# A linear-attention and two-MLP kernel: second w3 tile turned earlier, no weight tile begun in five steps, max product at full height

## The chip, the cores and the metric

The kernel runs on one core of one Trainium2 chip. The metric is the device time of one execution in microseconds; before the change it is 998.01 us, the median of 3 runs (996.71 to 998.25).

## The reference

```python
def phi(x):                                     # x: 4 x 8 x 576 x 64
    proj = np.einsum('bhsd,df->bhsf', x, w_phi) # f = 128
    proj = proj - np.max(np.abs(proj), axis=-1, keepdims=True)
    return np.concatenate([np.exp(proj), np.exp(-proj)], axis=-1)
q_p, k_p = phi(q), phi(k)
kv = np.einsum('bhsf,bhsd->bhfd', k_p, v)
z = np.sum(k_p, axis=2)
num = np.einsum('bhsf,bhfd->bhsd', q_p, kv)
den = np.einsum('bhsf,bhf->bhs', q_p, z)[..., None] + 1e-06
x = (num / den).transpose(0, 2, 1, 3).reshape(2304, 512)
h = ((x @ w1) * (x @ w2)) @ w3                  # 512x1024, 512x1024, 1024x1024
x = h @ w_out                                   # 1024 x 512
out = np.maximum(x @ w_in, 0.0) ** 2 @ w_out2   # 512x2048, 2048x512
```

The inputs of the attention are float32; the six MLP weights lie in DRAM as float64.

## The kernel before, in words

**Number forms.** A float32 product is made of three passes of a rounded form: a value is split into a high part (rounded by ScalarE, L142) and a low part (the rest, on VectorE or GpSimd, L143), and high x high, low x high and high x low are summed in PSUM (`passes`, `wide`). So a 512-wide contraction over 4 parts is 12 products. A float64 weight tile of 128x512 is decoded by integer work: its raw words are loaded by a DMA that SP issues (L99), ScalarE scales the high word (L106), VectorE makes the float's bits in four instructions (L108, L111; L115, L118), GpSimd adds (L123), and most tiles are then split (ScalarE L131, GpSimd L133). The generator `decoding` yields between these, so that the caller places them among other work.

**Attention.** 16 pairs of heads (`todo`, four batches by four pairs) run through a software pipeline: the loop over t issues, for every name in the list SLOT, one step of a pair that is t plus that step's offset. START is the same for the first slots. With `manual_schedule` the order in which the code issues is the order on each engine. The table `once` holds steps that run in one slot only; a step with offset -1 there runs in slot 15, with 0 in slot 16 (the pairs' last slot of work is 15; in slot 16 the last pair's `out` products and quotients remain). In a pair, `project_q` (L376) makes the projections of the queries in `pq`, 128 features x 1152 tokens in three banks. `max_q` takes maxima over blocks of 32 with a transposition within 32x32 squares (L383) into `m1`, 36 columns; `max_rows` transposes that on TensorE (L391) to 36 rows of `pm`; `max_parts` ends the maximum (L396), splits it, and two DMAs write its 1152 values as high and low row into `mrow`, a tile of two partitions. `minus_q` (L409) then adds a product of `minus`, 2 rows x 128 columns of -1, and the two rows of `mrow`, to each bank, so that every feature has its token's maximum taken off, and ScalarE takes the exponentials. In SLOT `minus_q` stands behind `turn_q1` or, in the last slots, `turn_w3`, and before `values1` (`pkv`, L428).

**First network.** The products with w3 and w_out are folded into one matrix first: for each of 8 chunks, two w3 tiles are turned on TensorE (`turn_weights`, L171), split (`keep`), and multiplied with w_out (`Fold.product`, L787); the split result `w3o` (`done`) then serves `yp` (L830). The 40 steps of the first network are 2 groups x 5 blocks of tokens (two of 512, one of 256, two of 512) x 4 chunks. A step makes `pa` and `pb` (x with w1 and w2), copies `a` (L902), multiplies (L910), splits, and issues the previous step's `yp`. Folds lie in steps 0 to 7. The first half of fold 0 was turned in slot 15 (`turn_w3`), the second is turned in step 0. The next block's x is loaded in a block's second step and split in three portions: part 0 in the third step, parts 1 and 2 and then 3 in the fourth (L143 on `c`). So steps 8 to 11 and 28 to 31 are the 256-wide block, with the splits of the 512-wide parts that follow in steps 10, 11 and 30, 31.

**Second network.** Step j of 16 in each block makes `ph` (x with w_in), on ScalarE and VectorE the squared ReLU (L971, L973; split L979, L981), and the products with w_out, `op` (L848), of the step before. In the first step the last block of the first network is emptied from PSUM too (`evict_second`, L816).

**Weights.** From slot 15 on `prefetch` loads raw tiles, and in each step of the MLPs `beat.rest(n)` finishes the tiles in hand and begins n new ones; their decode instructions stand between the step's own at `beat.one()` and behind it. The table `many` gives n by step index, 1 where it says nothing; room in the tile pool can hold a tile back (`begin`).

Of the kernel before, what the change touches and what calls it, by code (L numbers as in the profile page):

```python
# [9 lines left out]
F32 = mybir.dt.float32  # L10
F32R = mybir.dt.float32r
# [6 lines left out]
P = 128  # L18
C = 4
TAIL = 64  # L20
LEFT = 20
RIGHT = 13
# [11 lines left out]
tail_values/0  # L34
""".split()
SLOT = """
load_kq product_b project_k0 keep_values x_load project_q project_k1 less_max_k0 max_q turn_k out00 max_rows x_split0 max_parts w-1 store_x less_max_k1 x_split2 out01 exp_k0 x_split1 keep00 w1 high_k out10 keep01 turn_q0 out11 w1 keep_q0 project_k2 denominators0 keep10 w0 keep11 low_k less_max_k2 values0 gate turn_w3 exp_k1 denominators1 x_split3 exp_k2 w0 w0 w0 turn_q1 reciprocals keep_q1 minus_q product_a0 exp_q0 values1 exp_q1 turn_tails keep_tails split_q split_w3 low_tail low_q product_a1 quotients keep_a load_v tail_values
""".split()


# [1 line left out]
def attention_then_mlps(ctx: ExitStack, tc: tile.TileContext, q, k, v, w_phi, w1, w2, w3, wo, wi2, wo2, out):  # L42
    nc = tc.nc
    B, H, S, D = q.shape
# [17 lines left out]
    def unit(dtype, shape, name):  # L62
        return units.tile([P] + shape, dtype, tag="u", bufs=LEFT, name=name)
# [23 lines left out]
    def done_t(name):  # L87
        room_t[home_t.pop(name, 0)] += 1

    turn, room_t, home_t = [0], [2, 2], {}  # L90


    def decoding(src, name, got):
# [75 lines left out]
    def turn_weights(ps, w):  # L169
        for j in range(4):  # L170
            nc.tensor.transpose(ps[:, j * P:(j + 1) * P], w[:, j * P:(j + 1) * P], ident)  # L171
# [26 lines left out]
    with ExitStack() as actx:  # L198
        att = actx.enter_context(tc.tile_pool(name="att", bufs=2, side="right"))
        ps = actx.enter_context(tc.tile_pool(name="ps", bufs=3, space=PSUM))  # L200

        def bank(name, tag="t", bufs=3):
            return ps.tile([P, 512], F32, tag=tag, bufs=bufs, name=name)
# [2 lines left out]

        vs_t = [att.tile([P, 2, C, D + 1], F32, bufs=1, tag=f"vs{i}", name=f"vs{i}") for i in range(VS)]
        vt_t = [att.tile([P, NPR, 2, D + 1], F32, bufs=1, tag=f"vt{i}", name=f"vt{i}") for i in range(2)]
        for t in vs_t:
            nc.gpsimd.memset(t, 1.0)  # L210
        for t in vt_t:
# [167 lines left out]

        def max_q(z):  # L380

            z["m1"] = att.tile([P, 2 * nb], F32, tag="m1", name=f"m1_{z['nm']}")
            nc.vector.tensor_reduce(  # L383
                z["m1"].rearrange("p (i n) -> p i n", i=3), z["pv"].rearrange("p i (n r) -> p i n r", r=32),
                AX.X, ALU.max, apply_absolute_value=True, apply_transpose=True,
            )

        def max_rows(z):

            z["pm"] = bank(f"pm_{z['nm']}")[0:2 * nb, 0:P]  # L390
            nc.tensor.transpose(z["pm"], z["m1"], ident)  # L391

        def max_parts(z):
            pm = z["pm"]
            m = att.tile([2 * nb, 32], F32, tag="m", name=f"m_{z['nm']}")
            nc.vector.tensor_reduce(m, pm.rearrange("p (a r) -> p r a", a=4), AX.X, ALU.max)  # L396
            mh = att.tile([2 * nb, 2, 32], F32R, tag="mh", name=f"mh_{z['nm']}")
            nc.vector.tensor_copy(mh[:, 0], m)
            nc.vector.tensor_tensor(out=mh[:, 1], in0=m, in1=mh[:, 0].bitcast(F32), op=ALU.subtract)
            z["mrow"] = att.tile([2, 2 * S], F32R, tag="mrow", bufs=1, name=f"mrow_{z['nm']}")  # L400
            for s in range(2):
                nc.sync.dma_start(
                    z["mrow"][s:s + 1].bitcast(F32).rearrange("s (k r) -> s k r", r=32), mh[:, s].bitcast(F32)
                )
# [136 lines left out]
        beside += [decoding(*w3_of(i), w3s) for i in range(2)]  # L541
        beside.append(iter(()))
        load_kq(0)
        minus = att.tile([2, P], F32R, bufs=1, name="minus")
        nc.vector.memset(minus.bitcast(F32), -1.0)
        wst = att.tile([D, F], F32, bufs=1, name="wst")
        nc.sync.dma_start(wst, w_phi)
        wss = att.tile([P, 2, F], F32R, bufs=1, name="wss")
# [58 lines left out]
            first["g"] = unit(F32R, [2, 512], "g_0_0")  # L607
            split(first["g"], first["g32"], nc.vector)

        def turn_w3():  # L610
            first["w3T"] = unit(F32R, [2, 512], "w3T_0_0")
            first["pw3"] = bank("pw3_0_0")
            turn_weights(first["pw3"], w3s[0])

        once = {
            "turn_w3": (-1, turn_w3), "split_w3": (-1, lambda: split(first["w3T"], first["pw3"], nc.vector)),
            "x_load": (-3, lambda: load_x(0)),
            "product_a0": (-1, lambda: first_product("a", 0, range(KD - 1))),
            "product_a1": (-1, lambda: first_product("a", 0, range(KD - 1, KD))), "keep_a": (-1, first_a),
# [41 lines left out]
        return pool.tile([P, 512], F32, tag=tag, name=name)  # L661


    free = {"u": LEFT - 17, "w": RIGHT}
    home, given = {}, []

    def take(dtype, shape, name):
# [89 lines left out]
    class Fold:  # L757
# [4 lines left out]

        def turn(self):
            for g in range(2):
                if self.kc + g == 0:
                    continue
                self.ps[g] = bank_of(pre, "pre", f"pw3_{self.kc}_{g}")
                turn_weights(self.ps[g], w3s[2 * self.kc + g])
                done_t(w3_of(2 * self.kc + g)[1])

        def keep(self):
            for g in range(2):
                if g not in self.ps:
                    self.t.append(first["w3T"])
                    continue
                t = take(F32R, [2, 512], f"w3T_{self.kc}_{g}")
                split(t, self.ps[g], nc.vector)
                self.t.append(t)
# [19 lines left out]
    HG = NG // 2  # L798
    steps = [(grp, at, k) for grp in range(2) for at in range(len(order)) for k in range(HG)]
    folds = {i: i for i in range(NG)}  # L800
    many = {0: 3, 1: 3, 2: 2, 3: 2, 4: 2, 5: 2, 6: 2, 37: 2, 38: 2, 39: 2}
    mlp2 = mains + [tail]

    def evict_first(b, n, yp):
# [59 lines left out]
    with tc.manual_schedule(engines=mine):  # L864
# [5 lines left out]
        for s, (grp, at, k) in enumerate(steps):  # L870
# [23 lines left out]
                    blk.part = load_y_at(y_part, b, n, "yp")  # L894
            if s == 0:
                g = first["g"]
                beat.one()
            else:
                pa = bank_of(pre, "pre", f"pa_{b}_{c}")
                wide(pa, n, w12[2 * c], blk.cs)  # L900
                a_sb = lunit(F32, [512], f"a_{b}_{c}", "t", 2)
                nc.scalar.copy(a_sb[:, 0:n], pa[:, 0:n])  # L902
                pb = bank_of(pre, "pre", f"pb_{b}_{c}")
                wide(pb, n, w12[2 * c + 1], blk.cs)
                if at == B:
                    give(w12[2 * c], w12[2 * c + 1])
                if k == HG - 1:
                    col_split(x_in[nb_], nn, f"c{s}_{nb_}", [1, 2])
                g32 = lunit(F32, [512], f"g32_{b}_{c}", "g32", 2)
                nc.vector.tensor_tensor(out=g32[:, 0:n], in0=pb[:, 0:n], in1=a_sb[:, 0:n], op=ALU.mult)  # L910
                g = lunit(F32R, [2, 512], f"g_{b}_{c}", "g", 3)
                nc.scalar.activation(g[:, 0, 0:n], g32[:, 0:n], AF.Copy)  # L912
                beat.one()
                nc.vector.tensor_tensor(
                    out=g[:, 1, 0:n], in0=g32[:, 0:n], in1=g[:, 0, 0:n].bitcast(F32), op=ALU.subtract
                )
                if k == HG - 1:
                    nxt = col_split(x_in[nb_], nn, f"c{s}_{nb_}", [3])
                    give(*coming)
                    if nb_ == B and following[0] == 1:  # L920
                        give(xt)
# [27 lines left out]
        for at, (b, n) in enumerate(mlp2):  # L949
            cs, nt = nxt, n // P  # L950
            ops = None
            for j in range(NR):
# [43 lines left out]
                if j == NR - 2 and at < B:  # L996
                    col_split(x_in[nb_], nn, f"y{at}_{nb_}", [0])
                beat.tail()
                beat = beat.rest(1)
        last_product(prev)  # L1000


# [26 lines left out]
```

## Time and profile before

| | |
|---|---|
| median of 3 runs | 998.01 us (996.71 to 998.25) |
| the profiled execution | 996.72 us |
| its span, first to last instruction | 994.9 us |
| TensorE products, busy | 971.9 us, 98% |
| TensorE weight loads, busy | 813.8 us, 82% |
| VectorE, ScalarE, GpSimd, busy | 574.4, 412.0 and 253.8 us |
| mean granted TensorE clock | 0.992 |

Attention fills the span to about 225 us, the first network to about 587, the second the rest. The profile is of one execution; every row names an engine, the line of the kernel, the output and inputs of the instruction, and how many like it follow one another. In brackets stands the idle time of the engine just before, and what ended it. A row's length reaches from the start of its first instruction to the end of its last; products overlap, so the next row of the same engine can start before that end.

### The profile page before, as it was taken

The numbers are of one execution on the slowest core, as the hardware profiler recorded it, in microseconds if no ns is written. First come the engines' busy times: TensorE is split into PE (matmuls) and PEld (weight loads), VectorE is DVE, ScalarE is ACT, GpSimd is POOL, SyncE is SP. The second block draws the span as 40 slices with busy tenths as digits, with TensorE's granted clock in tenths as the row PEclk, the third lists the DMA queues.
The fourth block names the chain that finished last, engine by engine and source line by source line (L and its number), as shares of the span: only waits on it lengthen the run. The fifth ranks groups of instructions, "written<-read, shape, count | busy, mean of one in ns | idle before, by whom it ended". The sixth has DMA issues, their size and how long they took to land.

```text
span 994.9 us, 13026 instructions
## 1 busy us (share of the span) xinstructions
PE 971.9 (98%) x4944; PEld 813.8 (82%) x4944; DVE 574.4 (58%) x907; ACT 412.0 (41%) x785; POOL 253.8 (26%) x238
## 2 busy tenths in 40 slices
PE   7999999998999999999999989999999999999997
PEld 6888888886888888888888868888888888888896
DVE  5888888878765586467694398733223222322332
ACT  5887777763332343333332233423123222322322
POOL 3455555533321153233341055410000000000000
PEclk9999999998999999999999999999999999999999
DMA  6345444434332154451453343202000200100010
GB/s 175 97 130 141 128 137 124 138 107 148 106 106 66 62 173 131 142 182 64 153 195 127 127 137 97 85 1 85 1 1 21 65 1 0 64 1 1 1 43 22
DMA packets 68559, 89.11 MB, mean 90 GB/s; under 512 B 27984, under 2 KB 53136, under 8 KB 68496
## 3 DMA queue, kind: packets, MB, share of 16 engines
q1 hardware_dynamic: 68496, 88.28, 27.7%
q8 instruction: 39, 0.64, 0.3%
q14 instruction: 24, 0.20, 0.1%
HBM read 69.76 MB, written 18.35 MB: 89 GB/s over the span
## 4 chain that ended last, share of the span: by engine, by line
PE 92%; DVE 5%; issue 1%; DMA 1%; POOL 0%; ACT 0%; DVEq 0%; POOLq 0%
PE op L848 20%; PE ph L177 20%; PE pb L177 9%; PE pa L177 9%; PE yp L830 8%; PE po L452 6%; PE pkv L428 6%; PE pf L787 4%; PE pk L235 2%; PE pq L376 2%; PE pqt L307 1%; PE pq L409 1%; DVE c L143 1%; PE pkv L437 1%; PE pkt L290 1%
## 5 line engine op out<-in xcount | busy, mean ns | idle before, releaser
L848 PE MATMUL op<-w_w,r 128*128 128x512 f32 x864 | 215.6, 397 | 4.4 <-DVE yp L816 4.3
L848 PEld LDWEIGHTS op<-w_w,r 128*128 128x128 f32 x864 | 162.1, 189 | 42.2 <-issue 4.7
L973 DVE SCALAR_TENSOR_TENSOR r<-ph,t 128x512 f32<-128x512 f32 (+1 forms) x80 | 51.1, 638 | 200.2 <-ACT t L971 200.2
L177 PE MATMUL ph<-y,w_w 128*128 128x512 f32 (+1 forms) x768 | 166.2, 365 | 0.0
L177 PEld LDWEIGHTS ph<-y,w_w 128*128 128x128 f32 x768 | 133.3, 188 | 26.3
L971 ACT ACTIVATE t<-ph 128x512 f32<-128x512 f32 (+1 forms) x80 | 44.5, 557 | 223.1 <-PE ph L177 223.1
L830 PE MATMUL yp<-g,w3o 128*128 128x512 f32 (+1 forms) x480 | 107.4, 372 | 0.0
L123 POOL TENSOR_TENSOR dt_w<-dt_w,dy_w 128x512 f32<-128x512 f32 x48 | 63.5, 1323 | 154.8 <-DVE dy_w L118 141.2
L177 PE MATMUL pa<-c,w_w12a 128*128 128x512 f32 (+1 forms) x432 | 96.7, 370 | 3.4 <-DVE c L143 1.7
L830 PEld LDWEIGHTS yp<-g,w3o 128*128 128x128 f32 x480 | 83.6, 188 | 16.0
L177 PE MATMUL pb<-c,w_w12b 128*128 128x512 f32 (+1 forms) x432 | 93.9, 366 | 0.0
L177 PEld LDWEIGHTS pa<-c,w_w12a 128*128 128x128 f32 x432 | 74.9, 188 | 20.3 <-DVE c L143 3.9
L177 PEld LDWEIGHTS pb<-c,w_w12b 128*128 128x128 f32 x432 | 75.2, 188 | 13.4
L981 DVE TENSOR_TENSOR r<-r,r 128x512 fp32r<-128x512 f32 (+1 forms) x80 | 54.3, 679 | 42.7 <-ACT r L979 38.0
L910 DVE TENSOR_TENSOR g<-pb,a 128x512 f32<-128x512 f32 (+1 forms) x39 | 24.8, 636 | 84.8 <-PE pb L177 84.6
L979 ACT ACTIVATE r<-r 128x512 fp32r<-128x512 f32 (+1 forms) x80 | 47.2, 590 | 62.8 <-DVE r L973 62.8
L133 POOL TENSOR_TENSOR w_w<-dt_w,w_w 128x512 fp32r<-128x512 f32 x32 | 48.1, 1504 | 83.0 <-ACT w_w L131 83.0
L452 PE MATMUL po<-qp,kv 128*128 128x288 f32 x256 | 68.8, 406 | 0.0
L428 PEld LDWEIGHTS pkv<-vs,kp 128*128 128x128 f32 x512 | 60.9, 193 | 4.8 <-issue 2.0
L912 ACT ACTIVATE g<-g 128x512 fp32r<-128x512 f32 (+1 forms) x39 | 23.0, 589 | 96.7 <-DVE g L910 96.7
L428 PE MATMUL pkv<-vs,kp 128*128 128x65 f32 x512 | 62.8, 276 | 0.0
L902 ACT COPY a<-pa 128x512 f32<-128x512 f32 (+1 forms) x39 | 21.2, 543 | 82.1 <-PE pa L177 82.1
(130 smaller groups left out, 1408.8 us busy)
## 6 DMA issues: line engine op xcount, KB each, us to landing
x<-x_hbm SPq DMA_DIRECT2D x16, 512.0 KB
raw_w<-in_moe_w_dram SPq DMA_DIRECT2D x16, 512.0 KB
raw_w<-in_moe_w_in_dram SPq DMA_DIRECT2D x16, 512.0 KB
raw_w<-in_moe_w_out_dram SPq DMA_DIRECT2D x16, 512.0 KB
qm<-in_q_dram SPq DMA_DIRECT2D x16, 256.0 KB
km<-in_k_dram SPq DMA_DIRECT2D x16, 256.0 KB
vs<-in_v_dram SPq DMA_DIRECT2D x32, 128.0 KB
raw_wo<-in_moe_w_out_dram SPq DMA_DIRECT2D x8, 512.0 KB
```

Source lines behind the costliest of these rows:

```text
L123: nc.gpsimd.tensor_tensor(out=w, in0=t.bitcast(F32), in1=e.bitcast(F32), op=ALU.add)
L133: nc.gpsimd.tensor_tensor(out=dst[:, 1], in0=w[0], in1=dst[:, 0].bitcast(F32), op=ALU.subtract)
L177: nc.tensor.matmul(ps[:, 0:n], a, c, start=kk + i == 0, stop=kk == KD - 1 and i == 2)
L428: nc.tensor.matmul(z["pkv"][:, s, j], z["kp", j][:, c, s, :], z["vs"][:, j, c, :], start=j + s + c == 0, stop=False, skip_group_check=True,)
L452: nc.tensor.matmul(po[:, 0:HALF], z["kv"][:, e, j, :], z["qp"][:, e, j, s * HALF:(s + 1) * HALF], start=e == 0, stop=e == 1,)
L787: nc.tensor.matmul(pf, a, c, start=g + j + n == 0, stop=g == 1 and j == 3 and n == 2)
L830: nc.tensor.matmul(blk.yp[i][:, 0:blk.n], a, d, start=c % HG + s == 0, stop=c % HG == HG - 1 and s == 2)
L848: nc.tensor.matmul(ops[i], a, d, start=j + s == 0, stop=j == NR - 1 and s == 2)
L971: nc.scalar.activation(t[:, 0:n], ph[:, 0:n], AF.Relu)
L973: nc.vector.scalar_tensor_tensor(out=r32[:, 0:n], in0=ph[:, 0:n], scalar=0.0, in1=t[:, 0:n], op0=ALU.max, op1=ALU.mult)
L979: nc.scalar.activation(r[:, 0, 0:n], r32[:, 0:n], AF.Copy)
L981: nc.vector.tensor_tensor(out=r[:, 1, 0:n], in0=r32[:, 0:n], in1=r[:, 0, 0:n].bitcast(F32), op=ALU.subtract)
```

## The change

The max product gets 128 rows: `minus` has 128, and `mrow` is one tile of 128 partitions, zeroed once, of which the DMAs write the first two. `m1` is one of two fixed tiles of 128 columns, zeroed once, of which 36 are written, and the transposition makes 128 rows. The second w3 tile is turned and split in slot 16, ahead of the last pair's `out`. And `many` is 0 at 10, 11, 30, 31 and 40 (the first step of the second network, which now asks the table too).

```diff
 SLOT = """
-load_kq product_b project_k0 keep_values x_load project_q
+load_kq product_b project_k0 keep_values turn_w3b split_w3b x_load project_q
...
-    turn, room_t, home_t = [0], [2, 2], {}
+    turn, room_t, home_t = [0], [3, 2], {}
...
+        m1_t = [att.tile([P, P], F32, bufs=1, tag=f"m1{i}", name=f"m1_{i}") for i in range(2)]
+        mrow = att.tile([P, 2 * S], F32R, bufs=1, name="mrow")
...
-            z["m1"] = att.tile([P, 2 * nb], F32, tag="m1", name=f"m1_{z['nm']}")
+            z["m1"] = m1_t[z["pr"] % 2]
             nc.vector.tensor_reduce(
-                z["m1"].rearrange("p (i n) -> p i n", i=3), z["pv"].rearrange("p i (n r) -> p i n r", r=32),
+                z["m1"][:, 0:2 * nb].rearrange("p (i n) -> p i n", i=3), z["pv"].rearrange("p i (n r) -> p i n r", r=32),
...
-            z["pm"] = bank(f"pm_{z['nm']}")[0:2 * nb, 0:P]
+            z["pm"] = bank(f"pm_{z['nm']}")[:, 0:P]
             nc.tensor.transpose(z["pm"], z["m1"], ident)
...
-            pm = z["pm"]
+            pm = z["pm"][0:2 * nb]
...
-            z["mrow"] = att.tile([2, 2 * S], F32R, tag="mrow", bufs=1, name=f"mrow_{z['nm']}")
+            z["mrow"] = mrow
...
-        minus = att.tile([2, P], F32R, bufs=1, name="minus")
+        minus = att.tile([P, P], F32R, bufs=1, name="minus")
         nc.vector.memset(minus.bitcast(F32), -1.0)
+        for t in m1_t:
+            nc.vector.memset(t, 0.0)
+        nc.vector.memset(mrow.bitcast(F32), 0.0)
...
+            "turn_w3b": (0, lambda: turn_w3(1)), "split_w3b": (0, lambda: split_w3(1)),
...
-    free = {"u": LEFT - 17, "w": RIGHT}
+    free = {"u": LEFT - 18, "w": RIGHT}
...
         def turn(self):
             for g in range(2):
-                if self.kc + g == 0:
+                if self.kc == 0:
                     continue
...
-                    self.t.append(first["w3T"])
+                    self.t.append(first["w3T", g])
...
-    many = {0: 3, 1: 3, 2: 2, 3: 2, 4: 2, 5: 2, 6: 2, 37: 2, 38: 2, 39: 2}
+    many = {10: 0, 11: 0, 30: 0, 31: 0, 40: 0, 0: 3, 1: 3, 2: 2, 3: 2, 4: 2, 5: 2, 6: 2, 37: 2, 38: 2, 39: 2}
...
             if s == 0:
                 g = first["g"]
-                beat.one()
...
-                beat = beat.rest(1)
+                beat = beat.rest(many.get(len(steps) + 16 * at + j + 1, 1))
```

The order on TensorE around the end of attention, before. `pb_0_0` is a product of the first network's first step, `po` the last pair's `out`, `pw3_0_1` the turned second w3 tile, `pf_0` the first fold:

```order
L177 MATMUL pb_0_0_2697<-x_0_3_2642,w_w12b0_1702 128x512 x3
L452 MATMUL po_3_3_0_0_2713<-qp_3_3_2668,kv_3_3_2710 128x288 x2
L452 MATMUL po_3_3_0_1_2716<-qp_3_3_2668,kv_3_3_2710 128x288 x2
L452 MATMUL po_3_3_1_0_2721<-qp_3_3_2668,kv_3_3_2710 128x288 x2
L452 MATMUL po_3_3_1_1_2725<-qp_3_3_2668,kv_3_3_2710 128x288 x2
L171 MATMUL pw3_0_1_2774<-ident_69,dt_w3_1_2621 128x128 x4
L787 MATMUL pf_0_2782<-w_wo0_272,w3T_0_0_2633 128x512 x3
```

And of the change:

```order
L177 MATMUL pb_0_0_2671<-x_0_3_2616,w_w12b0_1688 128x512 x3
L171 MATMUL pw3_0_1_2688<-ident_69,dt_w3_1_2595 128x128 x4
L455 MATMUL po_3_3_0_0_2695<-qp_3_3_2642,kv_3_3_2684 128x288 x2
L455 MATMUL po_3_3_0_1_2698<-qp_3_3_2642,kv_3_3_2684 128x288 x2
L455 MATMUL po_3_3_1_0_2703<-qp_3_3_2642,kv_3_3_2684 128x288 x2
L455 MATMUL po_3_3_1_1_2707<-qp_3_3_2642,kv_3_3_2684 128x288 x2
L797 MATMUL pf_0_2754<-w_wo0_276,w3T_0_0_2607 128x512 x3
```

The four transpositions of the second tile have moved from behind the last pair's products to ahead of them.

ScalarE from the rounding of `g` to the copy of `a`, as the change has it; in the kernel before, the order is the same but that the rounding of `w3T_0_1` stands between `dy_w3_3` and `dy_w12a3`:

```order
L142 ACTIVATE w3T_0_1_2687<-pw3_0_1_2688 128x512
L463 COPY nd_3_3_2701<-po_3_3_0_0_2695 128x288
L463 COPY nd_3_3_2701<-po_3_3_0_1_2698 128x288
L463 COPY nd_3_3_2701<-po_3_3_1_0_2703 128x288
L463 COPY nd_3_3_2701<-po_3_3_1_1_2707 128x288
L142 ACTIVATE g_0_0_2716<-g32_0_0_2714 128x512
L106 ACTIVATE dy_w3_2_2748<-raw_w3_2_2667 128x512
L106 ACTIVATE dy_w3_3_2751<-raw_w3_3_2669 128x512
L106 ACTIVATE dy_w12a3_2789<-raw_w12a3_2729 128x512
L106 ACTIVATE dy_w3_4_2804<-raw_w3_4_2732 128x512
L106 ACTIVATE dy_w3_5_2807<-raw_w3_5_2798 128x512
L142 ACTIVATE w3o_0_2810<-pf_0_2754 128x512
L911 COPY a_0_1_2830<-pa_0_1_2817 128x512
```

The rounding of the second tile stands ahead of the four copies of `out` now; the conversions of w3_4 and w3_5 still stand ahead of the split of the fold and the copy of `a`.

VectorE in steps 10 and 11, before (`c` are the split parts of the block that begins in step 12, `w12b5` and `w12a6` the tiles begun in these steps):

```order
L910 TENSOR_TENSOR g32_4_2_3813<-pb_4_2_3800,a_4_2_3798 128x256
L108 TENSOR_SCALAR dt_w12b5_3783<-dy_w12b5_3782 128x512
L111 SCALAR_TENSOR_TENSOR dt_w12b5_3783<-raw_w12b5_3534,dt_w12b5_3783 128x512
L914 TENSOR_TENSOR g_4_2_3815<-g32_4_2_3813,g_4_2_3815 128x256
L143 TENSOR_TENSOR c10_2_0_3832<-x_2_0_3_3719,c10_2_0_3832 128x512
L115 TENSOR_SCALAR dy_w12b5_3782<-dt_w12b5_3783 128x512
L118 SCALAR_TENSOR_TENSOR dy_w12b5_3782<-raw_w12b5_3534,dy_w12b5_3782 128x512
L143 TENSOR_TENSOR c11_2_1_3874<-x_2_0_3_3719,c11_2_1_3874 128x512
L143 TENSOR_TENSOR c11_2_2_3877<-x_2_1_3_3720,c11_2_2_3877 128x512
L910 TENSOR_TENSOR g32_4_3_3880<-pb_4_3_3861,a_4_3_3859 128x256
L108 TENSOR_SCALAR dt_w12a6_3844<-dy_w12a6_3843 128x512
L111 SCALAR_TENSOR_TENSOR dt_w12a6_3844<-raw_w12a6_3643,dt_w12a6_3844 128x512
```

And of the change:

```order
L919 TENSOR_TENSOR g32_4_2_3784<-pb_4_2_3771,a_4_2_3769 128x256
L923 TENSOR_TENSOR g_4_2_3786<-g32_4_2_3784,g_4_2_3786 128x256
L143 TENSOR_TENSOR c10_2_0_3801<-x_2_0_3_3693,c10_2_0_3801 128x512
L143 TENSOR_TENSOR c11_2_1_3834<-x_2_0_3_3693,c11_2_1_3834 128x512
L143 TENSOR_TENSOR c11_2_2_3837<-x_2_1_3_3694,c11_2_2_3837 128x512
L919 TENSOR_TENSOR g32_4_3_3840<-pb_4_3_3821,a_4_3_3819 128x256
L923 TENSOR_TENSOR g_4_3_3842<-g32_4_3_3840,g_4_3_3842 128x256
L143 TENSOR_TENSOR c11_2_3_3845<-x_2_1_3_3694,c11_2_3_3845 128x512
L919 TENSOR_TENSOR g32_2_0_3891<-pb_2_0_3878,a_2_0_3876 128x512
L108 TENSOR_SCALAR dt_w12b5_3861<-dy_w12b5_3860 128x512
```

No decode stands between the splits any more; w12b5 is decoded in step 12. Steps 30, 31 and 40 lose their decode in the same way, and the tiles behind come later by up to three, until steps 36 to 38 begin the ones they began before; from step 40 on each tile of the second network is a step later.

## Rows read from the trace of the kernel before

**Rows 1.** Table of stretches: us, then each engine's busy time, granted clock, DMA.

```profile
30.00:218.00 188.00, 187.81 (x1288) 166.94 (x1288) 164.42 (x286) 151.00 (x307) 100.02 (x111) 1.00 0.46 132
...
232.00:234.00 2.00, 1.93 (x5) 1.54 (x6) 1.97 (x4) 0.00 (x0) 1.40 (x2) 0.50 0.12 47
...
594.00:596.00 2.00, 2.00 (x6) 1.53 (x5) 1.97 (x4) 0.47 (x1) 1.03 (x1) 0.50 1.04 406
```

**Rows 2.** Timeline of TensorE's products in one slot: start us, length us, work.

```profile
61.91 1.21 PE L376 MATMUL pq<-qT,wss 128*128 128x384 f32 x6
62.97 0.87 PE L235 MATMUL pk<-wbd,kT 128*128 128x256 f32 x6
...
67.13 0.60 PE L307 MATMUL pqt<-ident,qs 128*128 128x128 f32 x4
67.57 1.14 PE L452 MATMUL po<-qp,kv 128*128 128x288 f32 x4
...
68.89 1.89 PE L428 MATMUL pkv<-vs,kp 128*128 128x65 f32 x16
70.62 0.60 PE L307 MATMUL pqt<-ident,qs 128*128 128x128 f32 x4
71.16 0.79 PE L409 MATMUL pq<-mrow,minus 2*128 2x384 f32 x3
71.88 2.00 PE L428 MATMUL pkv<-vs,kp 128*128 128x65 f32 x16
```

**Rows 3.** Timeline of TensorE's weight loads in the same slot.

```profile
61.80 1.01 PEld L376 LDWEIGHTS pq<-qT,wss 128*128 128x128 f32 x6
...
71.16 0.47 PEld L409 LDWEIGHTS pq<-mrow,minus 2*128 2x128 f32 x3 [0.17 <-issue]
71.88 1.86 PEld L428 LDWEIGHTS pkv<-vs,kp 128*128 128x128 f32 x16 [0.26 <-issue]
```

**Rows 4.** Timeline of VectorE at the start.

```profile
4.29 0.69 DVE L282 TENSOR_TENSOR qs<-qm,qs 128x512 fp32r<-128x512 f32 x1 [2.76 <-ACT qs L278]
```

**Rows 5.** Timelines of TensorE, VectorE and ScalarE, 216 to 246 us.

```profile
218.69 2.99 PE L177 MATMUL pb<-x,w_w12b 128*128 128x512 f32 x12
221.52 4.04 PE L452 MATMUL po<-qp,kv 128*128 128x288 f32 x16
...
232.07 5.06 PE L787 MATMUL pf<-w_wo,w3T 128*128 128x512 f32 x11 [2.76 <-DVE w3T L143]
236.93 3.46 PE L177 MATMUL pa<-x,w_w12a 128*128 128x512 f32 x12
...
224.09 0.77 DVE L466 TRANSPOSE_TENSOR_REDUCE dc<-nd 64x18 f32<-64x576 f32 x1 [6.01 <-ACT nd L460]
...
239.72 0.70 ACT L106 ACTIVATE dy_w<-raw_w 128x512 f32<-128x512 f32 x1 [0.61 <-DMA raw_w<-in_moe_w_dram]
...
240.79 0.59 ACT L902 COPY a<-pa 128x512 f32<-128x512 f32 x1
```

**Rows 6.** Timeline of TensorE at step 12: the first and the next product.

```profile
359.50 2.58 PE L177 MATMUL pa<-c,w_w12a 128*128 128x512 f32 x9
...
364.25 2.00 PE L177 MATMUL pb<-c,w_w12b 128*128 128x512 f32 x8
```

**Rows 7.** Timelines of TensorE and VectorE at step 32.

```profile
511.29 1.32 PE L177 MATMUL pa<-c,w_w12a 128*128 128x512 f32 x5
...
517.34 1.99 PE L177 MATMUL pb<-c,w_w12b 128*128 128x512 f32 x8
...
510.06 1.54 DVE L115 TENSOR_SCALAR dy_w<-dt_w 128x512 int32<-128x512 int32 x1
```

**Rows 8.** Timelines of TensorE and VectorE at step 40.

```profile
592.18 4.58 PE L848 MATMUL op<-w_w,r 128*128 128x512 f32 x12 [4.31 <-DVE yp L816]
...
587.32 0.68 DVE L973 SCALAR_TENSOR_TENSOR r<-ph,t 128x512 f32<-128x512 f32 x1
...
589.68 1.76 DVE L981 TENSOR_TENSOR r<-r,r 128x512 fp32r<-128x512 f32 x1
```

More of the change, by code (lines that the diff above doesn't have):

```diff
@@ L36 @@
 SLOT = """
-load_kq product_b project_k0 keep_values x_load project_q project_k1 less_max_k0 max_q turn_k out00 max_rows x_split0 max_parts w-1 store_x less_max_k1 x_split2 out01 exp_k0 x_split1 keep00 w1 high_k out10 keep01 turn_q0 out11 w1 keep_q0 project_k2 denominators0 keep10 w0 keep11 low_k less_max_k2 values0 gate turn_w3 exp_k1 denominators1 x_split3 exp_k2 w0 w0 w0 turn_q1 reciprocals keep_q1 minus_q product_a0 exp_q0 values1 exp_q1 turn_tails keep_tails split_q split_w3 low_tail low_q product_a1 quotients keep_a load_v tail_values
+load_kq product_b project_k0 keep_values turn_w3b split_w3b x_load project_q project_k1 less_max_k0 max_q turn_k out00 max_rows x_split0 max_parts w-1 store_x less_max_k1 x_split2 out01 exp_k0 x_split1 keep00 w1 high_k out10 keep01 turn_q0 out11 w1 keep_q0 project_k2 denominators0 keep10 w0 keep11 low_k less_max_k2 values0 gate turn_w3 exp_k1 denominators1 x_split3 exp_k2 w0 w0 w0 turn_q1 reciprocals keep_q1 minus_q product_a0 exp_q0 values1 exp_q1 turn_tails keep_tails split_q split_w3 low_tail low_q product_a1 quotients keep_a load_v tail_values
 """.split()
@@ L608, in first_g, with turn_w3, split_w3 @@
             split(first["g"], first["g32"], nc.vector)
[L610 to L613, printed above, removed]
+        def turn_w3(g):
+            first["w3T", g] = unit(F32R, [2, 512], f"w3T_0_{g}")
+            first["pw3", g] = bank(f"pw3_0_{g}")
+            turn_weights(first["pw3", g], w3s[g])
+        def split_w3(g):
+            split(first["w3T", g], first["pw3", g], nc.vector)
         once = {
-            "turn_w3": (-1, turn_w3), "split_w3": (-1, lambda: split(first["w3T"], first["pw3"], nc.vector)),
+            "turn_w3": (-1, lambda: turn_w3(0)), "split_w3": (-1, lambda: split_w3(0)),
+            "turn_w3b": (0, lambda: turn_w3(1)), "split_w3b": (0, lambda: split_w3(1)),
             "x_load": (-3, lambda: load_x(0)),
```

## Prediction, made before the changed kernel was run

> **What bounds the kernel now.** The table of stretches by engine comes first, for who is the bound while attention runs: from 30 to 218 us TensorE is busy for 187.81 of 188 us at full clock, its weight loads for 167, VectorE for 164 and ScalarE for 151 [rows 1]. A gain there must shorten what TensorE runs. Then TensorE's timeline over the whole program, read for idle time in brackets and for the start of one group against the start of the next: the same products at the same size should take the same time everywhere, and where they don't, time is lost. At full clock twelve 512-column products take 221.52 - 218.69 = 2.83 us, 0.236 each [rows 5]. Last the timelines of the weight loads, VectorE and ScalarE at the places found, for what ended those waits.
>
> The profiled execution took 996.72 us, 1.3 under the median of 998.01. The sum is made against 996.72, and 1.3 is added at the end.
>
> **The max product at full height.** The three products of L409 have 2 rows of weights against 2 rows of data. From the start of the first (71.16) to the next group (71.88) is 0.72 us [rows 2]. Six products of the same 384 columns with 128 rows (L376) take 62.97 - 61.91 = 1.06, so 0.53 for three: 0.19 less. Two more places lose. From the four transpositions ahead of L409 to it is 71.16 - 70.62 = 0.54, while four such ahead of `out` take 67.57 - 67.13 = 0.44: 0.10. And the sixteen `pkv` products behind it read 2.00 us against 1.89 for sixteen elsewhere, of which I take 0.05, since the start of a row may hold the rest [rows 2]. The weight loads tell why: L376's first load is at 61.80, ahead of its product at 61.91, but L409's first load starts with its product at 71.16, after 0.17 idle that nothing but issue explains, and `pkv`'s first load after it waits 0.26 likewise [rows 3]. So a load is not taken ahead where 2-row and 128-row work meet, nor between the 2-row products. At 128 rows all loads should run ahead: 16 slots x (0.19 + 0.05) = 3.8, and 16 x 0.10, of which I take 1.4, as the row's DMA may be the last to come in a slot or two: **5.2 us less**. Floor: nothing. Ceiling: 16 x (0.19 + 0.11 + 0.10) = 6.4. It shows only if no other engine takes over; the nearest leave 21 us in 188 [rows 1], 1.3 a slot, and a slot gives 0.33.
>
> The Trainium skill, page "TensorE: Matmul & The Clock Gate", section "LDWEIGHTS (loading the stationary operand)", says that a load's time follows its columns and not its rows; its Part 3 adds that a load overlaps running products only where the row group differs. By that page this term would be nothing. The rows agree on the first point (0.47 us for three loads of 2 rows, 1.01 for six of 128) and not on the second: L376's loads, of one row group with what runs, start ahead of their products [rows 3].
>
> The wider `pm` (128 columns for 36) makes one load a little longer, under the `out` products: nothing. The row's DMAs are the same. At the start VectorE writes some 1,660 columns of constants more; at the 0.69 us that a split of 512 takes that is at most 2.2, and it stands idle for 2.76 before that split [rows 4]: nothing, and without that cover all 2.2.
>
> **The second w3 tile earlier.** TensorE stands 2.76 us before the second half of the fold (L787), because the tile's split on VectorE stands behind the last denominators and a decode. Then it runs at half clock: eleven products take 5.06 us, not 2.60, and the next twelve 3.46 against 2.99 [rows 5]; the granted clock there is 0.50, the level of 1.2 GHz [rows 1]. Lost: 2.76 + 2.46 + 0.47 = 5.7. The four transpositions move ahead of `out`, which comes 0.44 later and ends as before. The split goes into VectorE's 6.01 idle us before 224.09 [rows 5]. No DMA and no POOL instruction moves with it; on ScalarE its rounding passes the four copies of `out`, which today wait for TensorE anyway. Then the fold runs through: its first half ended at 232.07 - 2.76 = 229.31, eleven products more end near 231.7, step 1's two products (24 x 0.236) at 237.4. What is late next is the turn of the fourth w3 tile. It needs a bank that ScalarE frees by its copy of `a` (L902). That copy stands behind the conversions of w3_4 and w3_5, whose raw data SP asks for behind the store of the last quotients. The second conversion starts at 239.72 and the copy at 240.79 [rows 5]; with the quotients 0.44 later the copy ends near 240.79 + 0.59 + 0.44 = 241.8. So TensorE stands anew for 4.4 us. After 2.76 here and after 4.31 at step 40 the clock had fallen [rows 1]; there twelve products took 4.58 for 2.83, 1.7 more [rows 8]. New loss: 4.4 + 1.7 = 6.1 for 5.7. Taken, as the turn of w3 is partly done by then: **0.3 more**. Bounds: 5.7 less if the copy isn't waited for, 2.5 more if the raw data come 2 us later still.
>
> **No tile begun in steps 10, 11, 30, 31.** Behind the 256-wide block the first `pa` takes 364.25 - 359.50 = 4.75 us [rows 6] and 517.34 - 511.29 = 6.05 [rows 7], against 2.83: 1.9 and 3.2 lost to waits for the new block's parts. VectorE's splits of these stand behind decode (1.54 us at 510.06 and one more of 0.69, right ahead of the split that `pa` waits for [rows 7]); without it they run some 2 us earlier. At step 12 I take all: **1.9 less**. At step 32 the last split then ends within 0.1 us of its use, so **2.9 less**. Floor of each: a third, if ScalarE's roundings are late instead; ceiling: the whole. The decode comes up to three tiles later and has caught up by step 38; it falls into steps of twice the width.
>
> **No tile begun at step 40.** The first `op` waits 4.31 us for banks to be emptied [rows 8]. VectorE ends the first square at 587.32 + 0.68 = 588.0 and starts the low part at 589.68 [rows 8]; between stand two decode instructions. Without them the low part waits for ScalarE's rounding alone (about the 0.59 of its copies [rows 5]) and starts near 588.6. If it takes 1.76 as today [rows 8], or 0.69 as a split does when alone [rows 4], the emptying behind it is 1.1 to 2.1 earlier. Taken: **1.7 less**. The idle time left, 2.6, is near that of the fold, so the clock falls still. From here on tiles are a step later at most, with three steps of 24 products, 17 us, in reserve: nothing.
>
> **Sum.** -5.2 + 0.3 - 1.9 - 2.9 - 1.7 = -11.4: 985.3 in an execution like the profiled one, **986.6** as the median. Its own range is 983 to 990: 1 us each way for attention and for the boundaries, 2 for the fold.
>
> **The rivals.**
> - *The row count doesn't matter.* The gaps around L409 come from its change of operand or its semaphore, and stay. For: its three loads are no shorter or longer than others. Against: 128-row groups of other operands (turns, `out`, L376) follow one another without such a gap [rows 2, 3]. Then 986.6 + 5.2 = **991.8**. The page above sides with this one. Chance 0.2.
> - *The clock holds.* The idle left at step 40 or the fold leaves it at 2.4 GHz: 1.7 less at each, 986.6 - 3.4 = **983.2**, and 982 with attention at its ceiling. For: the 2.6 at step 40 is the shortest of these. Against: at 2.76 it fell [rows 1, 5]. Chance 0.12.
> - *The boundary waits move on.* The tiles not begun in 30 and 31 fall into steps 34 and 35, the next change of block, and cost there what they cost here: 986.6 + 4.8 = **991.4**. Against: those steps are twice as long. Chance 0.06.
> - *Slower: the fold waits for raw data.* From 237.4 on every us by which SP's loads for w3_4 and w3_5 land later is lost, with nothing to cover it, where today the slow first half hid it. Their last conversion starts at 239.72 now [rows 5]. Only if that came at 253.5 or after would the sum be over 2 us slower; at 255, 14.8 later than reckoned, 986.6 + 14.8 = **1001.4**. Against: what they queue behind moves by 0.44 only. Chance 0.02.
>
> **How the numbers follow.** The forecast has the other 0.6. A measurement of this kernel can tell about 0.2%, 2 us, from no change. The first and third rival together give 996.6, within that, and so does the first with the fold at its worst and one boundary at its floor: 0.04 of their chance is put there. Slower 0.02, faster 0.94. The range, 982 to 992, reaches over the held clock and the null in attention, and leaves out what lies beyond, under 2 in 10.
>
> **What would show it.** Right: L409 reads 128 rows, its loads start ahead of it, and from its start to `pkv` is 0.53; no idle before L787's second half; some 4 us of idle before the turn of w3 or `yp`, released by ScalarE; no waits in `pa` behind the narrow block; 2.6 before the first `op`. Wrong: still 0.7 at L409 (first rival); a clock of 1.00 behind the idle times (second); waits at steps 34 and 35 (third); `raw` conversions long after 240 (fourth); or VectorE as releaser inside attention, which none of them has.

## The result and the profile after

The changed kernel took 982.88 us in the median of four runs (982.80 to 984.67), the kernel before 997.36 beside it; the ratio is 0.9865, with a 95% interval of 0.984 to 0.9889, so 11 to 16 us less. Forecast were 986.6 within 982 to 992. The profiled execution's span is 981.0 us, 13.9 under the 994.9 of before.

The head of its page, and TensorE's longest waits (engine and line <- engine and line of what ended the wait: us in all, times, longest):

```profile
span 981.0 us, 13030 instructions
...
PE 961.5 (98%) x4944; PEld 813.3 (83%) x4944; DVE 571.6 (58%) x910; ACT 409.6 (42%) x785; POOL 252.6 (26%) x238
```

```profile
PE pw L171 <- POOL dt_w12a L123: 4.8, 1, 4.8
PE pkt L293 <- POOL vt L216: 4.3, 1, 4.3
PE op L858 <- DVE yp L826: 2.2, 1, 2.2
```

Line numbers here are those of the changed kernel: the max product, L409 before, is L412; `pkv` is L431 for L428, the fold L797 for L787, `op` L858 for L848. The text goes on calling the max product L409.

The wait at the start was there before. The waits of the fold (L787) and of `pa` behind the narrow blocks [rows 5 to 7] are gone, that of `op` is 2.2 for 4.31 [rows 8], and one of 4.8 is new. In attention, the stretch that answers to [rows 2], products first and then weight loads [rows 3]:

```profile
68.25 0.61 PE L310 MATMUL pqt<-ident,qs 128*128 128x128 f32 x4
68.61 0.77 PE L412 MATMUL pq<-mrow,minus 128*128 128x384 f32 x3
69.22 1.89 PE L431 MATMUL pkv<-vs,kp 128*128 128x65 f32 x16
70.95 0.28 PE L323 MATMUL ptt<-ident,qst 128*128 128x128 f32 x1
```

```profile
68.14 0.48 PEld L310 LDWEIGHTS pqt<-ident,qs 128*128 128x128 f32 x4
68.58 0.48 PEld L412 LDWEIGHTS pq<-mrow,minus 128*128 128x128 f32 x3
69.04 1.93 PEld L431 LDWEIGHTS pkv<-vs,kp 128*128 128x128 f32 x16
```

The loads carry no idle any more: the first load of the max product starts 0.03 ahead of its product, `pkv`'s 0.18 ahead. The way in, from the four transpositions to the max product, is 0.36 (0.54 before), from there to `pkv` are 0.61 (0.72), and `pkv` reads 1.89 (2.00). From one L409 to the second one after it, two slots, were 25.90 us, and are 25.16.

Around the end of attention (products, then ScalarE, VectorE and GpSimd):

```profile
214.90 0.60 PE L171 MATMUL pw<-ident,dt_w 128*128 128x128 f32 x4
215.34 4.05 PE L455 MATMUL po<-qp,kv 128*128 128x288 f32 x16
219.00 5.84 PE L797 MATMUL pf<-w_wo,w3T 128*128 128x512 f32 x24
...
230.13 0.60 PE L171 MATMUL pw<-ident,dt_w 128*128 128x128 f32 x4
235.51 1.09 PE L171 MATMUL pw<-ident,dt_w 128*128 128x128 f32 x4 [4.78 <-POOL dt_w12a L123]
236.25 4.10 PE L840 MATMUL yp<-g,w3o 128*128 128x512 f32 x12
...
233.74 0.66 ACT L106 ACTIVATE dy_w<-raw_w 128x512 f32<-128x512 f32 x1 [0.61 <-DMA raw_w<-in_moe_w_dram]
...
234.78 0.58 ACT L911 COPY a<-pa 128x512 f32<-128x512 f32 x1
...
234.92 0.69 DVE L143 TENSOR_TENSOR w3o<-pf,w3o 128x512 fp32r<-128x512 f32 x1 [0.94 <-ACT w3o L142]
...
234.12 1.26 POOL L123 TENSOR_TENSOR dt_w12a<-dt_w12a,dy_w12a 128x512 f32<-128x512 f32 x1 [1.88 <-DVE dy_w12a L118]
```

The fold runs through, and TensorE stands for 4.78 us at the turn of the fourth w3 tile. The trace names GpSimd's addition of another tile (`dt_w12a`) as what ended it; that and ScalarE's copy of `a` both end at 235.4, and by the code it is the copy that the turn needs, since it frees the bank. Behind it twelve products take 4.10 us instead of 3.0. The boundaries and the first `op`:

```profile
353.06 2.92 PE L177 MATMUL pa<-c,w_w12a 128*128 128x512 f32 x12
355.82 2.88 PE L177 MATMUL pb<-c,w_w12b 128*128 128x512 f32 x12
...
502.82 3.47 PE L177 MATMUL pa<-c,w_w12a 128*128 128x512 f32 x12
506.13 2.91 PE L177 MATMUL pb<-c,w_w12b 128*128 128x512 f32 x12
...
578.91 4.58 PE L858 MATMUL op<-w_w,r 128*128 128x512 f32 x12 [2.23 <-DVE yp L826]
```

Start to start, `pa` takes 2.76 at step 12 (4.75 in [rows 6]) and 3.31 at step 32 (6.05 in [rows 7]). Read at the same instruction of both traces, the lead of the changed kernel over the kernel before is 6.65 us when attention ends, 12.8 when the fold has run through, 6.44 behind its new wait, 8.43 behind step 12, 11.21 behind step 32, 13.27 at the first `op`; the last 0.6 come little by little over the 400 us of the second network, with no step that could be named.

### The profile page after: what moved, and what is told of

Same layout as the page of the kernel before. It is cut to its first block, busy times and chain, and to the rows that moved or that the text cites. A ratio compares the mean times of both kernels' runs of the same rounds, so it can differ in the third digit from the quotient of the medians.

```text
span 981.0 us, 13030 instructions
## 1 busy us (share of the span) xinstructions
PE 961.5 (98%) x4944; PEld 813.3 (83%) x4944; DVE 571.6 (58%) x910; ACT 409.6 (42%) x785; POOL 252.6 (26%) x238
## 4 chain that ended last, share of the span: by engine, by line
PE 93%; DVE 4%; issue 1%; POOL 0%; DMA 0%; ACT 0%; DVEq 0%; POOLq 0%
PE op L858 21%; PE ph L177 20%; PE pa L177 10%; PE pb L177 10%; PE yp L840 9%; PE po L455 6%; PE pkv L431 5%; PE pf L797 4%; PE pk L238 2%; PE pq L379 2%; PE pqt L310 1%; DVE dt_w L111 1%; PE pq L412 1%; PE pw L171 1%; PE pkt L293 1%
## 5 line engine op out<-in xcount | busy, mean ns | idle before, releaser
L858 PE MATMUL op<-w_w,r 128*128 128x512 f32 x864 | 215.1, 396 | 2.3 <-DVE yp L826 2.2
L858 PEld LDWEIGHTS op<-w_w,r 128*128 128x128 f32 x864 | 162.1, 189 | 39.7 <-ACT w_w L131 2.6
L990 DVE TENSOR_TENSOR r<-r,r 128x512 fp32r<-128x512 f32 (+1 forms) x80 | 51.0, 637 | 42.6 <-ACT r L988 37.9
L431 PEld LDWEIGHTS pkv<-vs,kp 128*128 128x128 f32 x512 | 61.3, 192 | 1.0 <-DVE kp L362 0.2
L431 PE MATMUL pkv<-vs,kp 128*128 128x65 f32 x512 | 60.6, 271 | 0.0
```

The source lines that it names most:

```text
L431: nc.tensor.matmul(z["pkv"][:, s, j], z["kp", j][:, c, s, :], z["vs"][:, j, c, :], start=j + s + c == 0, stop=False, skip_group_check=True,)
L858: nc.tensor.matmul(ops[i], a, d, start=j + s == 0, stop=j == NR - 1 and s == 2)
L990: nc.vector.tensor_tensor(out=r[:, 1, 0:n], in0=r32[:, 0:n], in1=r[:, 0, 0:n].bitcast(F32), op=ALU.subtract)
```

## The experiments

**One part at a time.** Three kernels hold one part each; the fourth holds the full-height tiles but uses 128 rows in slot 0 alone:

```diff
-            z["mrow"] = mrow
+            z["mrow"], z["high"] = mrow, P if z["before"] is None else 2
...
-                z["pv"][:, i], minus, z["mrow"][:, i * THIRD:(i + 1) * THIRD],
+                z["pv"][:, i], minus[0:z["high"]], z["mrow"][0:z["high"], i * THIRD:(i + 1) * THIRD],
```

The first (the lines on `m1`, `pm`, `mrow` and `minus`):

> The kernel before with the max product, its row and the maxima at full height, and nothing else of the change. Theory (the weight loads of 2-row products are not taken ahead): L409's start to pkv's start falls from 0.72 to about 0.6 us and the entry from 0.54 to 0.36 in each of 16 slots, 0.36 a slot, 5.4 us in all; with the clock at full level between 19 and 23 us as in the changed kernel another 1.6, so 7.0 us less than before, about 990.4. Rival (row count is no matter, the gain of the changed kernel in attention comes from its other parts): no difference, 997.4. The waits of the fold (2.8), of step 12 (1.1), of step 32 (2.2) and of step 40 (4.3) stay in both theories.

The second (`turn_w3b`, `split_w3b` and what goes with them):

> The kernel before with the second w3 tile turned and split in the last slot, and nothing else. Theory (the wait is moved, not removed): no idle before L787's second half, 4.4 to 4.8 us of idle at the turn of the fourth w3 tile, the clock at 0.50 behind it; the time within 0.5 us of before. Rival (the tile alone gives what the sum missed): 2 to 6 us less than before.

The third (`many`):

> The kernel before with no weight tile begun in steps 10, 11, 30, 31 and 40, and nothing else. Theory: 2.0 less at step 12, 2.7 at step 32, 2.1 at step 40, nothing lost later: 6.8 us less than before, about 990.6. Rival (the waits move on to the next block changes): less than 4 us gained, and idle of TensorE at steps 16, 20, 36.

The fourth:

> The kernel of e1_height, but with the product at full height in slot 0 alone; slots 1 to 15 use 2 rows of the same tiles. Theory A (the fall of the clock between 19 and 23 us belongs to slot 0's 2-row product): no fall, 1.6 + 0.36 = 2.0 us less than before. Theory B (the fall comes in some executions and not in others, whatever the product): 0.4 less in the median, and falls in some profiles of either form. In both, slots 1 to 15 show 0.72 at L409 again; if they don't, the zeroed tiles and not the row count matter.

| kernel | median, us | ratio to before (median 999.3, 23 runs) | in us |
|---|---|---|---|
| height alone (e1_height) | 991.91 | 0.9937 (0.9913 to 0.996) | 4.0 to 8.7 less |
| w3 tile alone (e2_turn) | 1000.47 | 1.0015 (0.9998 to 1.0032) | 0.2 less to 3.2 more |
| no begin alone (e3_no_begin) | 990.07 | 0.9919 (0.9901 to 0.9937) | 6.3 to 9.9 less |
| height in slot 0 alone (e7_slot0) | 997.59 | 1.0005 (0.9987 to 1.0022) | 1.3 less to 2.2 more |

The last column is the ratio times 999.3. The ratio is estimated over all runs and is not that of the two medians: executions of one kernel differ by up to 8 us, and for the last kernel the medians alone would say 1.7 less. The middles of the first three, -6.3, +1.5 and -8.1, sum to -12.9, which agrees with the whole change. The height alone has the slot of the changed kernel, 25.16 us for two: the gain belongs to it. The w3 tile alone gains nothing that can be measured; its wait is moved and is longer than the old one:

```profile
PE pw L171 <- ACT a L906: 4.8, 1, 4.8
...
PE op L853 <- DVE yp L821: 4.3, 1, 4.3
```

Here ScalarE's copy of `a` is named. With no tile begun, the waits at steps 12 and 32 are gone, that at step 40 is 2.2, and none appears at steps 16, 20 or 36, so that rival falls. With 128 rows in slot 0 alone, L409 takes 0.72 in the other slots, though it reads the same zeroed tiles. Of its theories on the clock, the 2.0 us less of the first lie outside the interval and the 0.4 of the second inside, but the spread above leaves little weight to that; the section on the hardware takes it up.

**How many rows it takes.** The kernel with the height alone, with 32 or 64 in place of `P` in two lines, and one with 2 rows in the product but the maxima's tile and transposition at full size. Each was timed once, so only their slots are read here:

```diff
-        mrow = att.tile([P, 2 * S], F32R, bufs=1, name="mrow")
+        mrow = att.tile([32, 2 * S], F32R, bufs=1, name="mrow")
...
-        minus = att.tile([P, P], F32R, bufs=1, name="minus")
+        minus = att.tile([32, P], F32R, bufs=1, name="minus")
```

> The kernel of e1_height with 32 rows of minus and of the row's tile in place of 128. Theory A (loads run ahead only where the row count is that of the neighbours, 128): L409's start to pkv's start stays 0.72 us, with idle ahead of its load and of pkv's. Theory B (only very few rows are in the way): 0.6 as with 128.

> The same with 64 rows. Theory A: 0.72 again. Theory C (the gap shrinks as rows are added): between 0.6 and 0.72.

> The kernel of e1_height with 2 rows in the product as before, so that only the maxima's tile and its transposition are at full width and height. Theory: the transposition's time under the out products is the same (next group 0.11 us after it in both), the slot as long as before, L409 to pkv 0.72: no gain. Rival (a narrow transposition costs as the 2-row product does): 0.1 to 0.2 us a slot gained.

Timelines of the weight loads with 32 and with 64 rows:

```profile
69.02 0.48 PEld L310 LDWEIGHTS pqt<-ident,qs 128*128 128x128 f32 x4
69.67 0.47 PEld L412 LDWEIGHTS pq<-mrow,minus 32*128 32x128 f32 x3 [0.17 <-issue]
70.39 1.86 PEld L431 LDWEIGHTS pkv<-vs,kp 128*128 128x128 f32 x16 [0.25 <-issue]
```

```profile
71.82 0.48 PEld L310 LDWEIGHTS pqt<-ident,qs 128*128 128x128 f32 x4
72.46 0.47 PEld L412 LDWEIGHTS pq<-mrow,minus 64*128 64x128 f32 x3 [0.17 <-issue]
73.18 1.86 PEld L431 LDWEIGHTS pkv<-vs,kp 128*128 128x128 f32 x16 [0.25 <-issue]
```

With 2, 32 and 64 rows the idle ahead of both loads is the same, L409 takes 0.72, and two slots 25.93 us; with 128 it is 0.61 and 25.16. So it is not a matter of few rows, and nothing shrinks on the way. The operands, the waits and the DMA are the same in all four, so the rival that the gap came with L409's operand or semaphore falls. The transposition at full size gains nothing (`out` follows it by 0.11 in both); two slots with it and 2 rows are even 0.03 longer than the 25.90 before.

That the change of the row count is what costs, and not a height under 128 as such, the second and third product of the group show. Their 32-row loads come behind products of 32 rows, and start 0.17 to 0.18 us ahead of their own products, while the product before is under way (which began at 69.67 and 69.95):

```profile
69.77 0.18 PEld L412 LDWEIGHTS pq<-mrow,minus 32*128 32x128 f32 x1
69.95 0.18 PEld L412 LDWEIGHTS pq<-mrow,minus 32*128 32x128 f32 x1
...
69.95 0.33 PE L412 MATMUL pq<-mrow,minus 32*128 32x384 f32 x1
70.13 0.33 PE L412 MATMUL pq<-mrow,minus 32*128 32x384 f32 x1
```

In the kernel before, the 2-row loads do the same: they start at 71.27 and 71.44, their products at 71.44 and 71.62. All three loads take the same tile, `minus`; small products of different operands in a row were not tried.

**The new wait at the fold, and the one left at step 40.** Four kernels on one chip: the changed kernel again; one that puts two conversions on ScalarE behind step 1's copy; one that also puts the fold's split ahead on VectorE, a decode behind, and `yp` ahead of the fourth tile's turn; and that with one tile less at step 39. The second, in `Beat`:

```diff
-            self.todo = [f for f in self.fresh for _ in range(2)]
+            self.todo = (self.fresh if held else []) + [f for f in self.fresh for _ in range(2)]
...
-            for f in coming[:2]:
-                advance(f)
-            return Beat(coming)
+            if not hold:
+                for f in coming[:2]:
+                    advance(f)
+            return Beat(coming, hold)
...
-            beat = beat.rest(many.get(s + 1, 1))
+            beat = beat.rest(many.get(s + 1, 1), s == 0)
```

The third adds to it (`owe` makes the late decode, `fold.done` is called after two steps of `todo`):

```diff
-                fold.turn()
-                fold.keep()
+                fold.turn([0] if s == 1 else range(2))
+                if s != 1:
+                    fold.keep()
...
+            if s == 1:
+                fold.turn([1])
+                fold.keep()
+                beat.owe()
...
+            if s == 0:
+                beat = beat.rest(many.get(s + 1, 1), fold.done)
+                fold = None
+            else:
+                beat = beat.rest(many.get(s + 1, 1))
```

And the fourth:

```diff
-    many = {10: 0, 11: 0, 30: 0, 31: 0, 40: 0, 0: 3, 1: 3, 2: 2, 3: 2, 4: 2, 5: 2, 6: 2, 37: 2, 38: 2, 39: 2}
+    many = {10: 0, 11: 0, 30: 0, 31: 0, 40: 0, 0: 3, 1: 3, 2: 2, 3: 2, 4: 2, 5: 2, 6: 2, 37: 2, 38: 2, 39: 1}
```

> The changed kernel once more, on the chip of the next three. The waits are the same to 0.1 us as in its first profile: 4.8 us at the turn of the fourth w3 tile, 2.2 before the first op. Theory A (the fall of the clock at 19 us needs the 2-row product): none at 19 us. Theory B (chance): a fall there in some profiles.

> The changed kernel, with the conversions of w3_4 and w3_5 on ScalarE put behind step 1's copy of a and rounding of g instead of ahead of them. Theory 1 (ScalarE's copy behind the raw data is what comes last, and the split of the fold on VectorE, behind the decode of w12a3, comes right after it): the turn of the fourth w3 tile starts when GpSimd has its tile, some 3 us earlier, but yp then waits for w3o's low part until about the time it starts now less 0.7; idle in two pieces, 3.5 to 4.3 us in sum, time within 1 us of the changed kernel. Theory 2 (only the copy was late): idle of 1.7 in all, 3 us or more gained.

> The changed kernel, with three things put in another order around step 1: the fold's split goes between the two decodes of step 0, the conversions of w3_4 and w3_5 and the decode of w12a3 behind step 1's own splits, and yp ahead of the turn of the fourth tile. Theory (the idle 4.8 us are made of things in the wrong order, and the clock behind them costs 1.2 to 1.7): idle under 1 us between step 1's pb and the second fold's products, clock 1.00 there, 4 to 6 us less than the changed kernel, about 0.9818 of the kernel before. Rival (VectorE has no room: the decode put off makes the second fold's turn late instead): less than 2 us gained, and a wait of pw or pf at step 2.

> The kernel of e8_fold, with one weight tile begun in step 39 instead of two, so that one decode less stands ahead of step 40's square and of the emptying of the banks. Theory: the emptying starts some 2 us earlier, the first op waits 0 to 0.5 us for 2.2, the clock stays up there: 2 to 4 us less than e8_fold, about 0.979 of the kernel before. Rival (the emptying itself, 2.5 us of VectorE behind the square, sets it): the wait stays above 1.5 us.

| kernel | median, us | ratio to before (median 997.93, 11 runs) |
|---|---|---|
| the change again (a2_change) | 982.60 | 0.9843 (0.982 to 0.9866) |
| conversions held (e10_held) | 980.49 | 0.9832 (0.98 to 0.9864) |
| fold in another order (e8_fold) | 981.07 | 0.9822 (0.9798 to 0.9847) |
| that, and one tile less at step 39 (e9_fold_evict) | 979.09 | 0.9801 (0.9776 to 0.9826) |

TensorE with the conversions held:

```profile
232.46 0.66 PE L171 MATMUL pw<-ident,dt_w 128*128 128x128 f32 x4 [1.55 <-POOL dt_w L123]
232.87 0.47 PE L842 MATMUL yp<-g,w3o 128*128 128x512 f32 x1
234.80 2.85 PE L842 MATMUL yp<-g,w3o 128*128 128x512 f32 x11 [1.45 <-DVE w3o L143]
```

So it was ScalarE's copy behind the raw data that held the turn: with that away it starts 3 us earlier, when its own tile is decoded, and VectorE's split is late next. Two pieces are left, 3.0 in sum for 4.8; 3.5 to 4.3 were expected. The third kernel has no idle there, but a wait at step 2 that is as long as those two:

```profile
249.44 1.02 PE L171 MATMUL pw<-ident,dt_w 128*128 128x128 f32 x4 [2.99 <-ACT a L929]
```

The rival was right: the decode that is put off comes to lie ahead of the next fold, and the 4 to 6 us that the theory expected did not come. What ends this wait are two things in a row:

```profile
246.32 1.31 POOL L123 TENSOR_TENSOR dt_w<-dt_w,dy_w 128x512 f32<-128x512 f32 x1 [1.89 <-DVE dy_w L118]
...
247.67 0.67 ACT L106 ACTIVATE dy_w<-raw_w 128x512 f32<-128x512 f32 x1 [4.34 <-POOL dt_w L123]
248.25 0.57 ACT L142 ACTIVATE w3o<-pf 128x512 fp32r<-128x512 f32 x1
248.73 0.57 ACT L929 COPY a<-pa 128x512 f32<-128x512 f32 x1
```

TensorE is idle from 246.45. GpSimd ends a w3 tile at 247.63, 1.2 us later; the other 1.8 pass until the copy of `a` ends at 249.30, which stands behind a conversion on ScalarE once more, this time one that waits for GpSimd. So only part of the 3 us is work owed by then; whether the rest would go with this conversion held too was not tried. With one tile less at step 39 the first `op` doesn't wait:

```profile
574.39 2.97 PE L177 MATMUL ph<-c,w_w 128*128 128x512 f32 x12
577.20 2.90 PE L876 MATMUL op<-w_w,r 128*128 128x512 f32 x12
```

What delayed the emptying of the banks was the decode ahead of it, and this wait's 2.2 us are gone. The intervals of the four overlap, but each contains the spread of the kernel before. Set against one another, the last kernel's four times (977.32 to 979.87) all lie under the five of the change (982.06 to 985.43), with medians 3.5 apart. Those of the third kernel do too, but only by 0.18 us at the nearest (979.46 to 981.88), and the second's (979.42 to 989.27) overlap, so for that one a gain is not shown.

## Why the prediction was right

| term, us | forecast | between the two profiles |
|---|---|---|
| attention, 16 slots | -5.2 | -5.0 over 14 of the slots |
| the clock at the start | not counted | -1.6 |
| second w3 tile | +0.3 | +0.2 |
| step 12 | -1.9 | -2.0 |
| step 32 | -2.9 | -2.7 |
| step 40 | -1.7 | -2.1 |

*Attention* went as said and for the reason given: at 128 rows the loads run ahead. The pieces were mis-sized against each other: the product itself gained 0.11 and not 0.19, since three products with full rows take 0.61, more than half of six at L376; the way in 0.18 and not 0.10, the way out 0.11 and not 0.05. A slot gained 0.37 between the two profiles, and 0.385 between 2 and 128 rows on one chip (the kernels with 128 rows in slot 0 alone and in all), against 0.33: that the errors of the pieces partly cancel is luck. The choice of 0.05 for the way out was a poor one: the `pkv` rows had shown 0.11. And one reading of the prediction was wrong, that loads are held up "between the 2-row products" too: there they run ahead, as the experiments show, so the time is lost mainly at the two changes of row count. On the rule of the Trainium skill's page "TensorE: Matmul & The Clock Gate", Part 3, that a load overlaps running products only where the row group differs, the measurement decides: `pkv`'s first load, of 128 rows, starts 0.18 ahead of its product, behind products of 128 rows. The Trainium skill's section "LDWEIGHTS (loading the stationary operand)" on the same page, by which a load's time goes by its columns and not by its rows, holds: three loads take 0.47 to 0.48 with 2, 32, 64 and 128 rows. The constants at the start are 1,408 columns, not some 1,660; they took 1.3 us, and VectorE still stood idle for 1.15 ahead of the split, so they cost nothing, as said.

*The fold* is the term that says most: a wait of 2.76 was taken away and 4.78 came in its place, for the reason that was named, and near the forecast size: 4.78 of wait and 1.4 of lower clock, for 4.4 and 1.7. The trace's own name for its cause was misleading in two of three profiles; moving the copy showed it. The second wait had a trace before the change already: in the two profiles with the old fold in which the clock held there (with the height alone, and with 64 rows), 1.1 us of it stand behind the first:

```profile
235.26 0.63 PE L171 MATMUL pw<-ident,dt_w 128*128 128x128 f32 x4 [1.11 <-POOL dt_w12a L123]
```

*The boundaries* gave 2.0 and 2.7 for 1.9 and 2.9; at step 32 0.5 us stays, for 0.3 reckoned. *Step 40*: VectorE's low part took 0.69, not 1.76, so the whole 2.1 came. No wait moved to steps 34 and 35. (The price of that rival, 4.8, held step 12's 1.9 as well; the tiles that it named would have given back 2.9.)

What was missing is the clock. The text priced a fall (from 2.4 to 1.2 GHz, 1.00 to 0.50 in the rows) as if it belonged to its wait, the same in each execution ("so the clock falls still"). It doesn't, as the last section shows. Of the 13.9 us between the two profiles, 11.4 were forecast; the other 2.5 are mostly the 1.6 at the start, where only the profile of before has a fall, 0.4 at step 40 and the 0.6 that has no place. The medians are 15.1 apart, counted from the 998.01 of the prediction; the profile of before was one of three in seven without a fall at step 32. The median of 982.88 lies nearer to the second rival's 983.2, the clock that holds, than to the forecast: at the 2.2 us left at step 40 the clock held in three of five profiles, though not in the one of the changed kernel read above. That the measured time lies in the range does not show the forecast's account of the clock.

## What to carry to other kernels

On TensorE a small product with fewer rows than its neighbours costs more than its columns: pad it with zeros to their height, if the tile and its rows of data can stay zeroed. Where a wait ends with a piece of work, look what is second in line on every engine before it is taken away; here it was longer than the first. Decode and other work that is due much later belongs in steps whose products cover it, not ahead of the work that a block change waits for.

## What the runs showed of the hardware

**The clock falls in some executions and not in others.** Here is the granted clock in stretches of 2 us (0.50 is 1.2 GHz) in the changed kernel's two profiles: us, then busy time of the five engines, the clock, DMA:

```profile
20.00:22.00 2.00, 2.00 (x20) 2.00 (x19) 0.00 (x0) 2.00 (x6) 0.19 (x1) 1.00 0.00 0
...
580.00:582.00 2.00, 2.00 (x6) 1.59 (x5) 1.97 (x4) 0.81 (x2) 0.56 (x1) 0.50 0.91 369
```

```profile
20.00:22.00 2.00, 2.00 (x11) 2.00 (x11) 0.00 (x0) 1.43 (x2) 0.00 (x0) 0.50 0.00 0
```

The second profile of the same kernel runs at half clock from 18 to 25 us, where the first doesn't, and not at step 40, where the first does. Over all 13 profiles, each kernel counted where it has the wait:

| place, wait of TensorE ahead of it | profiles with the clock at 0.50 behind it |
|---|---|
| start, slot 0's product with 128 rows | 2 of 7 |
| start, with 2, 32 or 64 rows | 5 of 6 |
| fold, 2.8 us in one piece | 5 of 7 |
| fold, 4.7 to 4.8 us | 3 of 3 |
| fold, 1.6 and 1.5 us in two pieces | 0 of 1 |
| step 2, 3.0 us | 1 of 2 |
| step 32, 2.2 us in four pieces | 4 of 7 |
| step 32, 0.3 us or less | 0 of 6 |
| step 40, 4.3 us | 7 of 7 |
| step 40, 2.2 us | 2 of 5 |
| step 40, none | 0 of 1 |

The stretches at 0.50 are 3 to 7 us long and cost half of that. They explain much of the spread of one and the same code: the kernels with 32 rows and with 2 rows and full maxima have the same slots and, behind slot 0, the same waits, but 992.5 and 996.6 us of span, and the second has some 10 us more at 0.50. So a wait costs its own length and a chance of a fall, by this table higher the longer it is; a single profile shows one draw. The start's fall doesn't need the 2-row product: two profiles with 128 rows have it. Whether its chance depends on the row count, 2 of 7 against 5 of 6 leave open, all the more as another thing differs there: how long slot 0's product waits for its row's DMA. Where that wait was 1.3 us or more (1.32 to 2.18), 5 of 6 profiles fell, at 1.05 or less 2 of 7, and the waits happened to be longer among those with few rows. No run separates the two.

**Partial heights are no cheaper than two rows.** Among neighbours of 128 rows, 2, 32 and 64 rows show the same 0.17 and 0.25 us of idle at the loads; only the full 128 ends them. Behind a product of its own 2, 32 or 64 rows, a load runs 0.17 to 0.18 us ahead of its product, as the full-height ones do.
